# Strassen's scheme for the first dense product of the last two blocks

## Chip, cores and metric

One Trainium2 chip, one core of it. The metric is the device time of one execution in microseconds. A chance or range in the prediction is for the median of such runs.

The engines by the profile's names: PE is the matmul engine (PEld its weight loads), DVE the vector engine, ACT the scalar engine, POOL GpSimd, SP the engine that issues nearly all DMAs. PE writes to PSUM only; the other engines carry results from PSUM to SBUF.

## The reference

Two layers, each an attention of 32 heads (Hedgehog features) followed by a dense block with a squared ReLU, on 2048 rows of 576 columns, all in float32:

```python
def _B_ref(x, w1, b1, w2, b2):             # D = 576, F = 4608
    h = jnp.einsum("bsd,df->bsf", x, w1) + b1
    r = jnp.where(h > zero, h, zero)
    h = r * r
    return jnp.einsum("bsf,fd->bsd", h, w2) + b2

x = A_x
x = x + _A_ref(_layernorm(x), A_wqkv, A_w_phi, A_wo)
x = x + _B_ref(_layernorm(x), B_w1, B_b1, B_w2, B_b2)
x = x + _A_ref(_layernorm(x), A_wqkv, A_w_phi, A_wo)
x = x + _B_ref(_layernorm(x), B_w1, B_b1, B_w2, B_b2)
```

`_A_ref` makes q, k, v, takes per head a small linear map and two softmaxes (of p and of -p) as features, sums features times v over all rows, and gives each row its query's share of these sums, times `wo`.

## The kernel before

**Blocks and order.** The 2048 rows are four blocks of TB = 512 (four tiles t of 128). K's sums need all rows, so a layer has a meeting point (`barrier`); behind it, the blocks are independent. Layer 1 runs them in the order 1, 0, 3, 2. For each block there is a dense block `g_mlp`, and beside it, by `weave`, the attention of the next block (`g_attend`): both are generators, and `weave` traces `rate` steps of the second for each `yield` of the first (36, one for each group f of 128 of the 4608 hidden features). In layer 1 the rate is 1.0, and the last dense block (block 2) has nothing beside it. Tile's planner then orders each engine's instructions: of those that its own estimate holds ready, the one traced first goes first, so the program's order is the priority. The order of an engine is fixed when the kernel is built.

**Precision.** A float32 product is made of three float32r products: each operand is split into a high part (ACT's `Copy` into float32r) and a low part (a subtraction of the high part from the raw value, on DVE or POOL), and hi*hi + hi*lo + lo*hi is summed.

**The dense block, per f** (`g_mlp`, L658 to L763). `first` loads 128 columns of w1 and 128 rows of w2 and splits them (L676, L677 on ACT; L679, L680 on DVE; L681 on POOL), one f ahead. `hidden` (L691) multiplies: D = 576 is four chunks of 128 and a tail of 64, which is stored twice so that one matmul of 128 rows does two of the three products; 5 + 4 + 5 = 14 matmuls with 512 moving columns, into one PSUM bank ("h"). `square` makes ReLU with bias, two squares (L698 to L700, ACT) and the low part (L701, DVE). `second` multiplies the previous f by w2: per tile t three matmuls of 448 columns (L718, `by_rows`), and three of 512 for the last 128 output columns (L709, `features`), into five PSUM banks acc0 to acc4. At the end the accumulators are added to the residual rows from `xm` and written out.

**Attention beside it** (`g_attend`): `g_q` loads the normalized rows back (`unspill`, L350, L351) and multiplies by the folded q weights (L363), 4 steps; `g_soft` (L398 to L407), 4 steps; `g_phi` (L558 to L568), 8 steps; `g_out`, which transposes (L598), multiplies by the sums (L614), then by `wo` (L645), adds the residual (L648) and calls `g_norm` for the dense block's operand. `held` puts the softmax and phi instructions of a step, on DVE, behind the last instruction of the newest `square` (L701). `g_norm` makes mean and variance, scales (L307, L308), transposes each tile on PE (L322, L332) and splits the result into the tiles `xh` and `xl`, which have two buffers.

Tiles in a pool with one tag share its buffers: a new tile of a tag waits until an old one is no longer read. PSUM has eight banks: "h", acc0 to acc4, and two of the tag "w" (`wtile`) for all else in layer 1's blocks.

Of the kernel before, what the change touches and what calls it, by code (L numbers as in the profile page):

```python
# [7 lines left out]
F32 = mybir.dt.float32  # L8
# [13 lines left out]
def layers_kernel(  # L22
# [35 lines left out]
    VW = DH + 1  # L58
    NQ = P // 32
# [13 lines left out]
    wf = dram.tile([D, 2 * D], F32, name="wf")  # L73

# [11 lines left out]
    def drain(gen):  # L86
        for _ in gen:
            pass
# [75 lines left out]
    vslots = [cst.tile([P, H * VW + 32 - VW], F32, name=f"vslot{t}") for t in range(NT)]  # L164
    for vt in vslots:
        nc.gpsimd.memset(vt[:, : H * VW].rearrange("p (h d) -> p h d", d=VW)[:, :, 0:1], 1.0)
        nc.gpsimd.memset(vt[:, H * VW :], 0.0)

# [122 lines left out]

    def g_norm(x_of, dst, name, then=None):

        xd = sb.tile([P, NT, 2, DT], F32, tag="xd", name=f"{name}e", bufs=1)

        def scale(t):
            x = x_of(t)
            stats = sb.tile([P, 2, 6], F32, tag="bns", name=f"{name}s{t}")
            mv = sb.tile([P, 2], F32, tag="bnm", name=f"{name}m{t}")
            rstd = sb.tile([P, 1], F32, tag="rstd", name=f"{name}d{t}")  # L300
            for h in range(2):
                nc.vector.bn_stats(stats[:, h, :], x[:, h * HP : (h + 1) * HP])
            nc.vector.bn_aggr(mv, stats.rearrange("p a b -> p (a b)"))
            nc.gpsimd.tensor_scalar(rstd, mv[:, 1:2], EPS, None, op0=ALU.add)
            nc.gpsimd.tensor_tensor(rstd, rstd, mhalf, op=ALU.pow)
            xn = sb.tile([P, KC * P], F32, tag="xn", name=f"{name}n{t}")
            nc.vector.tensor_scalar(xn, x[:, : KC * P], mv[:, 0:1], rstd, op0=ALU.subtract, op1=ALU.mult)  # L307
            nc.vector.tensor_scalar(xd[:, t], x[:, KC * P :].unsqueeze(1).to_broadcast([P, 2, DT]),  # L308
                                    mv[:, 0:1], rstd, op0=ALU.subtract, op1=ALU.mult)
            if then:  # L310
                then(t, x)
            return xn
# [139 lines left out]
    def sums_operands(layer):  # L452
        kv = sums[layer]["kv"]
        zb = cst.tile([P, 2, D], F32, name=f"zb{layer}", tag="zb")
        kbh = cst.tile([GW, 2, NG, GW], F32R, name=f"kbh{layer}", tag="kbh")
        kbl = cst.tile([GW, 2, NG, GW], F32R, name=f"kbl{layer}", tag="kbl")
# [116 lines left out]
    def g_out(layer, b, ph, dst, name, parts=1, pause=None, behind=None):  # L573
# [81 lines left out]
        yield from g_norm(x_after, dst, f"{name}n", keep)  # L655
# [109 lines left out]

    def load_x(b):
        def get(t):
            x = sb.tile([P, D], F32, tag="x", name=f"x0_{b}_{t}", bufs=5)
            nc.sync.dma_start(x, x_in[b * TB + t * P : b * TB + (t + 1) * P])
            return x  # L770
        return get

    def g_attend(layer, b, x, raws, dst, name, behind=None):
# [9 lines left out]
        yield from g_out(layer, b, ph, dst, name, behind=behind and behind["last"])  # L783
# [63 lines left out]
    for layer in range(2):  # L847
# [4 lines left out]
        for i, b in enumerate(order):  # L852
            n = f"{layer}_{b}"
            nxt = {}
            keep = {}

            def g_back(i=i, prev_rows=prev_rows, keep=keep, nxt=nxt, nxt_raws=nxt_raws):
# [16 lines left out]
                if i + 1 < NB:  # L874
                    yield from g_attend(layer, order[i + 1], None, nxt_raws, nxt, f"a{layer}_{order[i + 1]}",
                                        dense if i == 0 else None)

            rows = []
            weave(g_mlp(layer, b, ready, rows, f"m{n}", None if i else dense["turned"]), g_back(), 1.0 if layer or i == 0 else 1.5)
# [37 lines left out]
```

## Time and profile before

| what | us |
|---|---|
| median of 3 runs (2570.54 to 2573.32) | 2571.38 |
| profiled execution, its own time | 2570.54 |
| its span (first to last instruction) | 2568.5 |
| layer 1, dense block 1 with attention of block 0 | 1510 to 1780 |
| dense block 0 with attention of block 3 | 1780 to 2056 |
| dense block 3 with attention of block 2 | 2056 to 2331 |
| dense block 2 alone | 2331 to 2568 |

A profile shows for each engine when an instruction ran and what it waited for. "Busy" of PE is the time covered by matmuls, whose ends are modelled; the distance from one matmul's start to the next is the better measure of its cost. An idle engine costs nothing unless the end waits for it, so the first question to each view is which engine has no idle time in the stage at hand.

### The profile page before, as it was taken

Reading aid. Unit: us, or ns where it says so; the run is one execution under the profiler, and the core shown is the slowest. Engines: PE = TensorE matmul, PEld = TensorE weight load, DVE = VectorE, ACT = ScalarE, POOL = GpSimd, SP = SyncE. Lnnn points to the kernel's source line nnn. Section 1 sums busy time; section 2 is a strip of 40 time slices with the busy share of each in tenths; the row PEclk is TensorE's granted clock in tenths of the full one; section 3 lists DMA queues with packets and bytes.
Section 4 is the critical chain, followed back from the end, with each engine's and each line's share of the span. In section 5 each row is a group of like instructions: output and inputs, shape, how many; then the busy total and the mean of one; then the engine's idle time right before and its main releaser. Section 6 shows DMA issues by size and latency. Waiting matters only on the chain.

```text
span 2568.5 us, 41275 instructions
## 1 busy us (share of the span) xinstructions
PE 2525.1 (98%) x15456; PEld 2230.4 (87%) x15456; DVE 1456.0 (57%) x2246; ACT 1235.5 (48%) x2061; POOL 634.9 (25%) x645
## 2 busy tenths in 40 slices
PE   8998999999999999999999999999999999999999
PEld 8998888888888888888888988888888888888887
DVE  7778844456665467556434788444663458444333
ACT  4344554445554455545544445535555445534544
POOL 3444311113222133223111433121231213121111
PEclk9999999999999999999999999999999999999999
DMA  8103333354333533343333123334432343234332
GB/s 251 57 23 92 102 111 91 109 185 128 92 93 113 172 126 97 88 133 103 110 101 101 43 90 108 106 103 158 128 103 84 108 160 107 84 101 130 99 101 77
DMA packets 298018, 280.59 MB, mean 109 GB/s; under 512 B 28186, under 2 KB 238362, under 8 KB 295770
## 3 DMA queue, kind: packets, MB, share of 16 engines
q1 hardware_dynamic: 296560, 275.26, 35.3%
q10 hardware_dynamic: 1258, 2.70, 0.3%
q8 instruction: 121, 1.98, 0.3%
q14 instruction: 79, 0.65, 0.1%
HBM read 246.90 MB, written 30.97 MB: 108 GB/s over the span
## 4 chain that ended last, share of the span: by engine, by line
PE 56%; DVE 3%; ACT 1%; issue 0%; DMA 0%; POOL 0%; DVEq 0%; ACTq 0%; SPq 0%; POOLq 0%
PE m_1ph L691 8%; PE m_0ph L691 6%; PE m_1acc L718 6%; PE m_0acc L718 5%; PE m_2ph L691 5%; PE m_3ph L691 4%; PE m_3acc L718 3%; PE m_2acc L718 3%; PE m_1acc L709 2%; PE m_0acc L709 1%; PE m_2acc L709 1%; PE m_3acc L709 1%; PE a_2po L645 1%; PE t1opo L645 1%; PE k_0kp L363 1%; PE t1pv L363 1%
## 5 line engine op out<-in xcount | busy, mean ns | idle before, releaser
L718 PE MATMUL m_1acc<-m_1s,m_1hb 128*128 128x448 f32 x864 | 199.3, 366 | 1.5 <-DVE m_1hb L701 1.5
L718 PE MATMUL m_0acc<-m_0s,m_0hb 128*128 128x448 f32 x864 | 199.4, 366 | 1.3 <-DVE m_0hb L701 1.3
L718 PE MATMUL m_3acc<-m_3s,m_3hb 128*128 128x448 f32 x864 | 199.7, 366 | 1.0 <-DVE m_3hb L701 1.0
L718 PE MATMUL m_2acc<-m_2s,m_2hb 128*128 128x448 f32 x864 | 199.4, 366 | 1.3 <-DVE m_2hb L701 1.3
L691 PE MATMUL m_0ph<-a_0nh,m_0h 128*128 128x512 f32 (+1 forms) x760 | 192.8, 383 | 0.2 <-DVE m_0h L679 0.2
L691 PE MATMUL m_2ph<-a_2nh,m_2h 128*128 128x512 f32 (+1 forms) x760 | 192.0, 382 | 0.2 <-DVE m_2h L679 0.2
L718 PEld LDWEIGHTS m_0acc<-m_0s,m_0hb 128*128 128x128 f32 x864 | 161.9, 188 | 23.2 <-DVE m_0hb L701 2.2
L718 PEld LDWEIGHTS m_1acc<-m_1s,m_1hb 128*128 128x128 f32 x864 | 162.0, 188 | 22.9 <-DVE m_1hb L701 2.3
L718 PEld LDWEIGHTS m_2acc<-m_2s,m_2hb 128*128 128x128 f32 x864 | 161.9, 188 | 22.8 <-DVE m_2hb L701 2.2
L718 PEld LDWEIGHTS m_3acc<-m_3s,m_3hb 128*128 128x128 f32 x864 | 161.8, 188 | 22.6 <-DVE m_3hb L701 1.4
L679 DVE TENSOR_TENSOR m_2h<-m_2r,m_2h 128x640 fp32r<-128x640 f32 x72 | 61.8, 858 | 181.6 <-ACT m_2h L676 179.5
L691 PEld LDWEIGHTS m_2ph<-a_2nh,m_2h 128*128 128x128 f32 x760 | 136.9, 188 | 26.7 <-DVE m_2h L679 0.7
L691 PEld LDWEIGHTS m_0ph<-a_0nh,m_0h 128*128 128x128 f32 x760 | 136.6, 188 | 26.8 <-DVE m_0h L679 0.7
L679 DVE TENSOR_TENSOR m_3h<-m_3r,m_3h 128x640 fp32r<-128x640 f32 x72 | 65.6, 912 | 157.1 <-ACT m_3h L676 147.9
L679 DVE TENSOR_TENSOR m_1h<-m_1r,m_1h 128x640 fp32r<-128x640 f32 x72 | 64.9, 903 | 155.4 <-ACT m_1h L676 149.3
L679 DVE TENSOR_TENSOR m_0h<-m_0r,m_0h 128x640 fp32r<-128x640 f32 x72 | 64.7, 899 | 153.9 <-ACT m_0h L676 148.5
L681 POOL TENSOR_TENSOR m_2s<-m_2r,m_2s 128x128 fp32r<-128x128 f32 x72 | 60.7, 844 | 361.7 <-ACT m_2s L677 343.2
L681 POOL TENSOR_TENSOR m_0s<-m_0r,m_0s 128x128 fp32r<-128x128 f32 x72 | 59.5, 826 | 351.7 <-ACT m_0s L677 318.5
L681 POOL TENSOR_TENSOR m_3s<-m_3r,m_3s 128x128 fp32r<-128x128 f32 x72 | 58.5, 813 | 341.8 <-ACT m_3s L677 321.8
L681 POOL TENSOR_TENSOR m_1s<-m_1r,m_1s 128x128 fp32r<-128x128 f32 x72 | 59.7, 829 | 322.4 <-ACT m_1s L677 312.8
L698 ACT ACTIVATE m_3hr<-m_3ph,b1t 128x512 f32<-128x512 f32 x72 | 49.4, 687 | 186.6 <-PE m_3ph L691 181.7
L698 ACT ACTIVATE m_0hr<-m_0ph,b1t 128x512 f32<-128x512 f32 x72 | 49.4, 686 | 176.2 <-PE m_0ph L691 173.6
(1507 smaller groups left out, 6381.0 us busy)
## 6 DMA issues: line engine op xcount, KB each, us to landing
m_3r<-in_B_w SPq DMA_DIRECT2D x72, 288.0 KB
m_2r<-in_B_w SPq DMA_DIRECT2D x72, 288.0 KB
m_0r<-in_B_w SPq DMA_DIRECT2D x72, 288.0 KB
m_1r<-in_B_w SPq DMA_DIRECT2D x72, 288.0 KB
m_3r<-in_B_w SPq DMA_DIRECT2D x72, 256.0 KB
m_2r<-in_B_w SPq DMA_DIRECT2D x72, 256.0 KB
m_0r<-in_B_w SPq DMA_DIRECT2D x72, 256.0 KB
m_1r<-in_B_w SPq DMA_DIRECT2D x72, 256.0 KB
```

Source lines behind the costliest of these rows:

```text
L363: nc.tensor.matmul(pt[:, :HP], a, m, start=(k == 0), stop=(k == len(ops) - 1))
L645: nc.tensor.matmul(pt[:, :HP], a, m[:w, g], start=(g == 0 and k == 0), stop=(g == NG - 1 and k == 2))
L679: nc.vector.tensor_sub(l1, r1, h1.bitcast(F32))
L681: nc.gpsimd.tensor_sub(s2[:, D + R : 2 * D], r2[:, R:], s2[:, R:D].bitcast(F32))
L691: nc.tensor.matmul(ph[:, cols], a, m, start=(k == 0), stop=(k == len(ops) - 1))
L698: nc.scalar.activation(hr, ph, AF.Relu, bias=b1t[:, f : f + 1])
L709: nc.tensor.matmul(acc[KC], a, m, start=(f == 0 and k == 0), stop=(f == NF - 1 and k == 2))
L718: nc.tensor.matmul(acc[t][:, :R], a[:, rows], m, start=(f == 0 and k == 0), stop=(f == NF - 1 and k == 2))
```

## The change

The dense blocks of blocks 3 and 2 are no longer two runs of `g_mlp` but one generator, `g_pair`. For two groups f0, f1 (a pass k, 18 of them) and both blocks, the first product is a 2x2 by 2x2 product of blocks: the weights w1 cut in K into halves of 288 (HP) and in features into f0, f1 (a11, a12 for f0; a21, a22 for f1); the normalized rows cut in K and into block 3 (b11, b21) and block 2 (b12, b22). The scheme (Winograd's form of Strassen's) makes seven products:

- of weights: a11, a12, s1 = a21+a22, s2 = s1-a11, s4 = a12-s2, s3 = a11-a21, a22
- of rows: b11, b21, t1 = b12-b11, t2 = b22-t1, b22, t3 = b22-b12, t4 = b21-t2

and sums them in three PSUM banks: bx = a11*b11, then + s2*t2, + s3*t3, + a22*t4; by = a12*b21, then s4*b22; bz = s1*t1. Each product has 7 matmuls of 512 columns: K of 288 is two chunks of 128 and 32 rows, which stand three times in one operand of 96 rows (TP) so that one matmul does all three partial products.

Second products: block 3's follows in the passes as before (`second`); block 2's squared hidden values are written to DRAM (`hd`, 36 tiles of 256 KB), and when block 3 is done, its 36 second products follow alone with w2 loaded once more.

The rows' sums t1 to t4 are made where the rows are normalized: `g_norm_first` (block 3) writes its operand to DRAM (`pth`, `ptl`, `ptt`); `g_norm_second` (block 2) loads it and makes the sums (`combine`: DVE and POOL) and their splits. For that, both attentions must be done before `g_pair`: they now both run beside block 0's `g_mlp`, at 2.2 steps an f in place of 1.0. The weights' sums and splits are made by `split_pair` one pass ahead. Many operands live in buffers of other tags (`zb`, `xd`, `kbh`, `kbl`, the v slots, `E`, `ft`, `whi`, `wraw`, `x`, `qk`).

The core of the diff:

```diff
+    def new_slot(t, name, dtype=F32):
+        return cst.tile([P, NC * P], dtype, name=name, tag=f"vslot{t}")
...
+    def g_norm_halves(x_of, name, then, main, tail):
+        xd = sb.tile([P, NT, 2 * TP], F32, tag="xd", name=f"{name}e", bufs=1)
+        xns = []
+        for t in range(NT):
+            x = x_of(t)
+            mv, rstd = moments(x, t, name)
...
+            yield
+        for t in range(NT):
+            pt = wtile(f"{name}p{t}")
...
+            main(t, p4)
+            yield
+            if t % 2:
+                pt = wtile(f"{name}p{NT}{t}")
+                p3 = pt[:TP].rearrange("p (a n) -> p a n", a=2)
+                for a in range(2):
+                    for i in range(2):
+                        nc.tensor.transpose(p3[:, a, i * P : (i + 1) * P],
+                                            xd[:, t - 1 + i, a * TP : (a + 1) * TP], ident)
+                tail(t // 2, p3)
+                yield
...
+        def combine(new, c11, c21):
+            b12, b22 = new
+            temps = [sb.tile([P, D], F32, tag="x", name=f"{name}u{i}", bufs=5) for i in range(2)]
...
+            nc.vector.tensor_sub(t1, b12, c11[0])
+            if len(c11) > 1:
+                nc.vector.tensor_sub(t1, t1, c11[1])
+            nc.vector.tensor_sub(t2, b22, t1)
+            nc.vector.tensor_copy(t3, b12)
+            nc.vector.tensor_sub(t3, b22, t3)
+            nc.gpsimd.tensor_sub(t4, c21[0], t2)
+            if len(c21) > 1:
+                nc.gpsimd.tensor_add(t4, t4, c21[1])
+            return (("b22", b22), ("t1", t1), ("t2", t2), ("t3", t3), ("t4", t4))
+        def main(t, p4):
...
+            for k, src in combine((p4[:, 0], p4[:, 1]), *old):
+                hi, lo = (p[:, :, rows] for p in ops[k][:2])
+                nc.scalar.activation(hi, src, AF.Copy)
+                (nc.vector if k == "b22" else nc.gpsimd).tensor_sub(lo, src, hi.bitcast(F32))
...
+    def g_pair(layer, blocks, x, after, name):
...
+            def split(key, src):
+                op = homes[key].rearrange("p (c n) -> p c n", c=NC)
+                hi, lo = op[:, : HK + 1], op[:, HK + 1 :]
+                nc.scalar.activation(hi, src, AF.Copy)
+                nc.vector.tensor_sub(lo, src[:, :HK], hi[:, :HK].bitcast(F32))
+                band = slice(2 * TW, 3 * TW)
+                nc.gpsimd.tensor_sub(hi[band, HK], src[band, HK], hi[band, HK].bitcast(F32))
+                wops[k, key] = (hi, lo)
+
+            split("a11", a11)
+            split("a12", a12)
+            nc.gpsimd.tensor_add(ss[0], a21, a22)
+            split("s1", ss[0])
+            nc.gpsimd.tensor_sub(ss[1], ss[0], a11)
+            split("s2", ss[1])
+            yield
+            nc.gpsimd.tensor_sub(ss[3], a12, ss[1])
+            split("s4", ss[3])
+            nc.gpsimd.tensor_sub(ss[2], a11, a21)
+            split("s3", ss[2])
+            split("a22", a22)
...
+        def product(k, ps, key, op, start):
+            hi, lo = wops.pop((k, key))
+            xh, xl, xtail = x[op]
+            ms = [(hi[:, c], xh[:, c]) for c in range(HK)] + [(hi[:TP, HK], xtail)]
+            ms += [(hi[:, c], xl[:, c]) for c in range(HK)]
+            ms += [(lo[:, c], xh[:, c]) for c in range(HK)]
+            for i, (a, m) in enumerate(ms):
+                nc.tensor.matmul(ps, a, m, start=start and i == 0, stop=i == len(ms) - 1, skip_group_check=True)
...
+        drain(split_pair(0, load_pair(0)))
+        raw = load_pair(1)
+        for k in range(NP):
+            f0, f1 = 2 * k, 2 * k + 1
+            prep = split_pair(k + 1, raw) if k + 1 < NP else iter(())
...
+            load_wide(f0)
+            product(k, bx, "a11", "b11", True)
+            product(k, by, "a12", "b21", True)
+            z = sb.tile([P, TB], F32, tag="hr", name=f"{name}z{f0}", bufs=2)
+            nc.scalar.activation(z, by, AF.Copy)
+            nc.vector.scalar_tensor_tensor(z, bx, bias(f0), z, op0=ALU.add, op1=ALU.add)
+            nc.scalar.activation(z, z, AF.Relu)
+            square(f0, z)
+            product(k, bz, "s1", "t1", True)
+            next(prep, None)
+            product(k, bx, "s2", "t2", False)
...
+            nc.scalar.activation(v, bz, AF.Copy)
+            nc.vector.tensor_add(u, bx, v)
+            product(k, by, "s4", "b22", True)
+            product(k, bx, "s3", "t3", False)
+            nc.vector.scalar_tensor_tensor(u, by, bias(f0), u, op0=ALU.add, op1=ALU.add)
+            nc.vector.scalar_tensor_tensor(v, bx, bias(f1), v, op0=ALU.add, op1=ALU.add)
+            nc.scalar.activation(u, u, AF.Relu)
+            nc.scalar.activation(u, u, AF.Square)
+            nc.sync.dma_start(hd[f0], u)
+            keep_high(f1, v)
+            if k:
+                second(f0 - 1)
+            load_wide(f1)
+            product(k, bx, "a22", "t4", False)
+            drain(prep)
+            z = sb.tile([P, TB], F32, tag="hr", name=f"{name}z{f1}", bufs=2)
+            nc.scalar.activation(z, bx, AF.Relu, bias=bias(f1))
+            square(f1, z)
+            if k + 2 < NP:
+                raw = load_pair(k + 2)
+            second(f0)
+            yield
+        last_rows(0)
...
+        for f in range(NF, 2 * NF - 1):
+            second(f)
+            if f + 2 < 2 * NF:
+                load_wide(f + 2)
+                load_high(f + 2)
+            yield
+        last_rows(1)
...
         for i, b in enumerate(order):
...
+            if layer and i == 2:
+                drain(g_pair(layer, order[2:], operands, rows, f"m{n}"))
+                break
...
+                if layer and i == 1:
+                    for j, norm in ((2, g_norm_first), (3, g_norm_second)):
+                        yield from g_attend(layer, order[j], None, None, operands, f"a{layer}_{order[j]}", None, norm)
...
-            weave(g_mlp(layer, b, ready, rows, f"m{n}", None if i else dense["turned"]), g_back(), 1.0 if layer or i == 0 else 1.5)
+            weave(g_mlp(layer, b, ready, rows, f"m{n}", None if i else dense["turned"]), g_back(), 1.0 if i == 0 else 2.2 if layer else 1.5)
```

The functions used there and not shown: `load_pair` loads 256 columns of w1 in two halves of K (the 32 tail rows four times, side by side in 128 partitions); `load_wide` loads and splits 128 rows of w2, as `first` did; `square`, `features`, `by_rows`, `second` and `last_rows` are those of `g_mlp` with an index for the block; `load_high` loads a tile of `hd` and splits it.

246 lines of the change are left out of this document (226 added, 20 removed).

## The prediction

> **What bounds the kernel now.** I read the page first: busy shares, then the chain of waits.
>
> ```profile
> span 2568.5 us, 41275 instructions
> PE 2525.1 (98%) x15456; PEld 2230.4 (87%) x15456; DVE 1456.0 (57%) x2246; ACT 1235.5 (48%) x2061; POOL 634.9 (25%) x645
> ```
>
> PE is busy for 98% of the span. Then the stages that change, by windows: layer 1's second, third and fourth blocks (columns: us, then PE, PEld, DVE, ACT, POOL busy, clock, DMA share, GB/s).
>
> ```profile
> 1780.00:2056.00 276.00, 275.63 (x1404) 240.62 (x1403) 149.50 (x226) 136.39 (x221) 59.27 (x61) 1.00 0.39 119
> 2056.00:2331.00 275.00, 273.89 (x1395) 238.69 (x1394) 147.46 (x226) 133.61 (x218) 58.33 (x62) 1.00 0.36 109
> 2331.00:2568.00 237.00, 232.41 (x1097) 200.56 (x1095) 82.45 (x124) 112.97 (x180) 32.83 (x36) 1.00 0.35 104
> ```
>
> The first two hold a dense block and the next block's attention, the last a dense block alone. And all that PE waited for after 1510 us, by the view of waits (total, times, longest):
>
> ```profile
> PE m_1acc L718 <- DVE m_1hb L701: 1.0, 1, 1.0
> PE t1onp L322 <- DVE t1onn L307: 0.9, 1, 0.9
> PE a_2np L322 <- DVE a_2nn L307: 0.7, 1, 0.7
> PE a_3np L322 <- DVE a_3nn L307: 0.4, 1, 0.4
> PE a_0np L322 <- DVE a_0nn L307: 0.4, 1, 0.4
> ```
>
> 3.4 us in 1058: these stages are bound by PE's own work. So matmuls taken out come off the end one for one, as long as the other engines still stay hidden. Every new stall comes on top.
>
> **Step 1, the first product: -28.9 us.** For two groups f of 128 hidden features and two blocks, `hidden` issues 2x2x14 = 56 matmuls; seven `product` calls issue 7x7 = 49, of the same 128x512 form (K is 256 + 96 stacked rows instead of 512 + 64 doubled). The chain shows one `hidden` of 14, in two alternating lengths:
>
> ```profile
> 2401.28 3.26 PE m_2ph L691 x14
> 2407.66 3.17 PE m_2ph L691 x14
> ```
>
> Mean 3.215 us, 0.2296 each. 18 passes x 7 = 126 fewer: 28.9 us. The second products stay: 72 x 15 matmuls.
>
> **Step 2, transposes: +1 us.** The tail of K is now transposed by halves: 8 transposes a block for 4, so 8 more for two blocks.
>
> ```profile
> 1783.10 0.66 PE a_0np L322 x4
> ```
>
> 0.165 each, 1.3 us by this row and less within a run of them: I take 1.
>
> **Step 3, two attentions within one dense block: +18 us.** Both attentions now run beside block 0's `g_mlp` at 2.2 steps an f. One attention has 39 steps (4 q, 4 softmax, 8 phi, 13 in `g_out`, 10 in the norm), two 78, and 36 x 2.2 = 79. PE's work only moves. DVE's is the question; four windows of one answer:
>
> ```profile
> 2360.00:2550.00 190.00, 190.00 (x871) 163.27 (x870) 64.32 (x90) 94.63 (x150) 27.02 (x30) 1.00 0.33 95
> 1827.00:1905.00 78.00, 78.00 (x357) 66.66 (x356) 65.03 (x90) 42.28 (x66) 28.47 (x25) 1.00 0.35 103
> 663.00:725.00 62.00, 60.92 (x289) 52.21 (x288) 58.52 (x83) 35.96 (x55) 24.97 (x21) 1.00 0.38 110
> 1470.00:1480.00 10.00, 6.39 (x33) 6.16 (x32) 10.00 (x17) 1.30 (x4) 5.00 (x4) 0.66 0.32 90
> ```
>
> Row one is the dense block alone: 30 f's, so 6.33 us of PE and 64.32/30 = 2.14 us of DVE each. Row two is softmax and phi of one attention at 1.0 step an f: 65.03 - 78/6.33 x 2.14 = 38.7 us of DVE for the attention. Softmax, phi and the empty step behind are 13 steps: at 2.2 they span 5.9 f's, 37.4 us of PE, while DVE needs 38.7 + 5.9 x 2.14 = 51.3. It is short by 13.9 us. `held` puts each step's DVE work behind the last square of its f, and the following f's weight and square subtractions queue behind it; those are late next, and PE waits for them as it did at L701. PE can run ahead by about one `hidden` (3.2 us) to one f (6.3), and instructions of coming f's slip into gaps of the chain. I take 9 a time, 18 for two. Lower bound, row three: at 1.5 steps an f, DVE busy 58.52 of 62, PE lost 62 - 60.92 = 1.1: 2 us for two. Upper: all of it, 28. The attention's ACT work there is 42.28 - 12.3 x 94.63/30 = 3.5 us and its POOL work 28.47 - 12.3 x 27.02/30 = 17.4, both far under 37.4. In `g_out` DVE has room and the order recovers, but a PE idle time is not won back.
>
> **Step 4, between the two attentions: 0 us.** Normalized block 3 goes out by three transfers (2.4 MB), and only then does block 2's come in (2.3 MB), since xh and xl have two buffers and block 0 holds one. What one load takes, from its issue on SP to the first q product:
>
> ```profile
> 1777.35 0.38 SPq L350 DMA_DIRECT2D a_3uh<-xth  x1
> 1790.25 0.42 PE L363 MATMUL a_3qp<-a_3q0h,a_3uh 128*128 128x288 f32 x2
> ```
>
> 13 us at most, perhaps 20 with the store: three f's of `g_mlp`, whose matmuls can fill it; the four q steps (14 us of PE) then come without f's between. Without that cover it costs 13. On SP the loads of coming f's (issued one f ahead) must get past these waits.
>
> **Step 5, the hand-over to `g_pair`: +7 us.** The old hand-overs cost PE 0.4 and 0.7 (L322 above). Now, behind the last step, `xd` must be free before half of the first weights loads, `full` (in vslot0 and 1, the homes of a11 and a12) must be read, and POOL has a queue: a `main` gives it six 128x256 operations, four mains and two tails 26, then split_pair(0) four sums and seven bands. POOL's prices (lines; mean ns behind the busy time):
>
> ```profile
> L652 POOL TENSOR_TENSOR a_3x<-a_3x,b2t 128x576 f32<-128x576 f32 x4 | 5.7, 1432 | 2.9 <-DVE a_3ne L308 2.9
> L249 POOL TENSOR_TENSOR w0v0l<-fv,w0v0h 128x288 fp32r<-128x288 f32 x5 | 4.0, 796 | 6.9 <-ACT w0v0h L248 6.9
> L681 POOL TENSOR_TENSOR m_2s<-m_2r,m_2s 128x128 fp32r<-128x128 f32 x72 | 60.7, 844 | 361.7 <-ACT m_2s L677 343.2 <-issue 18.4
> L304 POOL TENSOR_SCALAR n_0d<-n_0m 128x1 f32<-128x1 f32 x4 | 0.9, 221 | 6.8 <-DVE n_0m L303 6.8
> ```
>
> At 0.8 the 26 take 21 us in a stretch that PE crosses in 6/2.2 f's, 17 us, and a few transposes: 2 to 4 late. Then s1 needs two bands, a sum, ACT's copy and its band, about 3.5 us; each further sum with copy and band about 2 against the 1.6 of a product. a11 and a12 (3.2 us) cover part. I take 8, less one old hand-over: 7; from 1 (all ready in time) to 13 (26 x 0.8 - 17, 3.5 and 7 x 0.844, uncovered).
>
> By the clock: row four above is a stretch with one PE wait of 3.6 us (L500, the longest of all); the granted clock there is 0.66, 3.4 us lost in 10. The Trainium skill (TensorE: Matmul & The Clock Gate, What's actually happening) says that a window of about 3.4 us without work halves the clock; the trace agrees, and by that rule one unbroken wait of 7 us would make the sum 3 higher.
>
> **Step 6, the pair loop: +5 us.** A pass has 49 + 30 matmuls: 49 x 0.2296 + 2 x (6.33 - 3.215) = 17.5 us. Against it (rows of the dense block alone, of the fold, and of a block's end):
>
> ```profile
> L701 DVE TENSOR_TENSOR m_2hb<-m_2hr,m_2hb 128x512 fp32r<-128x512 f32 x30 | 20.8, 693 | 10.8 <-ACT m_2hr L700 10.8
> L680 DVE TENSOR_TENSOR m_2s<-m_2r,m_2s 128x448 fp32r<-128x448 f32 x30 | 18.8, 626 | 20.3 <-ACT m_2s L677 20.3
> L241 DVE TENSOR_TENSOR w0k0l<-fo,w0k0h 128x288 fp32r<-128x288 f32 x5 | 2.2, 445 | 0.0
> L676 ACT ACTIVATE m_2h<-m_2r 128x640 fp32r<-128x640 f32 x30 | 21.9, 729 | 0.0
> L677 ACT ACTIVATE m_2s<-m_2r 128x576 fp32r<-128x576 f32 x30 | 20.6, 686 | 20.5 <-PE m_2acc L709 19.5 <-DVE m_2hb L701 1.0
> L699 ACT ACTIVATE m_2hb<-m_2hr 128x512 fp32r<-128x512 f32 x30 | 18.6, 621 | 0.0
> ```
>
> DVE: 7 x 0.42 (128x256, just under L241) + 2 x 0.63 + 6 x 0.69 = 8.3 us. ACT: 7 x 0.53 (128x384, down the slope from L676 to L699) + 2 x 0.69 + 12 x 0.63 = 12.7. POOL: 4 x 1.0 (128x384, between L249 and L652) + 2 x 0.84 + 7 bands of 32x128, from 0.22 (L304) to 0.84: 7.2 to 11.6. Nobody exceeds PE. s2 must wait until DVE has read bx: copy 0.62 + 0.69 and handovers against s1's 1.6 us, so it has no slack; I take 0.3 a pass, 5 us, from 0 to 18 x 0.69 = 12. Queued behind that DVE read are u, v and coming weights, a pass ahead. SP: 1.9 MB a pass, 106 GB/s, against 279 shown below; a store of `hd` waits for ACT with coming loads behind it, also a pass early.
>
> POOL and DVE get in each other's way; from the timeline:
>
> ```profile
> 689.02 1.44 POOL L558 TENSOR_TENSOR a_0m<-a_0Q0e,zb 128x576 f32<-128x576 f32 x1
> 689.20 1.74 DVE L680 TENSOR_TENSOR m_2s<-m_2r,m_2s 128x448 fp32r<-128x448 f32 x1
> ```
>
> The subtraction that takes 0.63 took 1.74: POOL began 0.18 us before, and it ended 0.48 after POOL. The Trainium skill (SBUF — State Buffer, Who interferes with whom) has the rule: a DVE instruction with two inputs in SBUF and a GpSimd instruction that reads SBUF exclude each other. The trace agrees; this is rival B's mechanism.
>
> **Step 7, block 2's second product alone: +2 us.** An f now has 3.1 us of PE against ACT 0.69 + 0.62, DVE 0.63 + 0.69 in turn behind it, 2.6 in all: it fits by half a microsecond, with 544 KB per 3.1 us, 179 GB/s, below what this row shows:
>
> ```profile
> 1780.00:1800.00 20.00, 19.63 (x139) 18.59 (x138) 11.09 (x23) 8.35 (x16) 4.46 (x6) 1.00 0.82 279
> ```
>
> From 0 to 36 x 0.3 = 10. **Sum:** -28.9 + 1 + 18 + 0 + 7 + 5 + 2 = +4. The profiled execution took 2570.54 us, 2 more than its span, and lies 0.8 below the median: 2574.5, as a median 2575.4.
>
> **Rivals.** A, the order absorbs DVE's shortage as at 1.5 steps an f (1.1 each): step 3 costs 2, the sum is -12, 2559. For it speaks row three, where DVE had nothing to spare and PE lost almost nothing; against it, that there DVE's need (38.7 + 9.8 f's x 2.14 = 59.7) still fitted into 62. B, the shared access binds the pair loop: DVE's two-input work (7 x 0.42 + 2 x 0.63 + 2 x 0.69 = 5.6 us) excludes POOL's. With bands at 0.84 and sums at 1.43 POOL has 13.3; 18.9 against 17.5 is 1.4 a pass, 25 for 18 in place of 5: 2595. It decides once POOL is above 11.9. C, the transfers between the attentions aren't covered, since SP stands in wait while block 0's weights queue behind: +13, 2588.
>
> **The numbers.** Forecast 0.45 (2575, its own range 2564 to 2588), A 0.33, B 0.14, C 0.08. About 0.2%, 5 us, can be told from no change. Faster by more: A nearly whole and a bit of the forecast, 0.34; within: 0.20; slower: 0.46. The range takes A with less in steps 5 and 6 (2549) and most of B: 2549 to 2600.
>
> **What would show it.** Step 1: 882 first-product matmuls at 0.23 for 1008. Step 3: PE waits for DVE L701's and L679's likes, twice, about 9 us each, in block 0's softmax and phi; none, and A is right. Step 4: idle before the second q products. Step 5: one PE stall of 5 to 10 us before s1, ended by POOL or ACT. Step 6: passes of 17.5 to 18 us; 19 with POOL over 70% busy is B. Step 7: 3.1 us an f. The prediction is wrong if step 3 or 5 costs nothing, or if a wait not listed costs over 10 us.

## The result and the profile after

| | us |
|---|---|
| before, median of 4 runs (2570.54 to 2573.32) | 2571.79 |
| after, median of 4 runs (2591.81 to 2594.93) | 2593.59 |
| ratio, with its 95% interval | 1.0084 (1.0067 to 1.0102) |
| span of the profiled execution, before and after | 2568.5 and 2590.1 |

The change makes the kernel 22 us slower, 0.8%, and clear of the runs' spread. In the experiments below, one execution of t4_dve took 4970 us where its other four took 2581 to 2584; it is left out of that kernel's ratio, and its cause is open. The first page of the profile after, span and busy times:

```profile
span 2590.1 us, 41423 instructions
PE 2519.7 (97%) x15282; PEld 2211.0 (85%) x15282; DVE 1533.6 (59%) x2408; ACT 1266.7 (49%) x2177; POOL 797.6 (31%) x869
```

PE has 174 instructions fewer than before. That is the 126 of step 1, plus 56 since block 3's and block 2's first two f's had been multiplied in halves (2 x 2 x 14 more matmuls) and the pair has none of these, less the 8 transposes of step 2. The work has gone as forecast; the span has grown in spite of it. All that PE waited for over 1 us after 1510 us, from the view of waits (total, times, longest):

```profile
PE m_0ph L708 <- DVE m_0h L696: 7.4, 4, 2.7
PE a_2pt L615 <- DVE a_2Q3e L585: 5.0, 1, 5.0
PE a_2np L805 <- DVE a_2nl L904: 3.3, 1, 3.3
PE m_0py L771 <- DVE a_2nl L904: 2.7, 1, 2.7
PE m_3px L988 <- DVE m_3wv L954: 2.5, 1, 2.5
PE m_3py L988 <- ACT m_3wv L953: 1.9, 1, 1.9
PE m_3px L988 <- DVE m_3u L1089: 1.5, 1, 1.5
PE a_2np L805 <- DVE a_2nh L877: 1.3, 1, 1.3
PE m_3py L988 <- POOL m_3wv L956: 1.1, 1, 1.1
```

The first two rows belong to softmax and phi of the two attentions, the others to the norm that feeds the pair and to the pair's first pass. The windows put them in their places (us, then PE, PEld, DVE, ACT, POOL busy, clock, DMA share, GB/s):

```profile
1820.00:1840.00 20.00, 17.28 (x74) 14.40 (x73) 19.06 (x24) 12.81 (x19) 8.71 (x7) 0.91 0.17 47
1840.00:1860.00 20.00, 16.10 (x63) 12.28 (x62) 19.45 (x34) 6.77 (x11) 10.06 (x8) 0.91 0.21 63
2000.00:2020.00 20.00, 18.68 (x85) 15.62 (x84) 19.88 (x33) 10.15 (x17) 9.50 (x8) 1.00 0.28 79
2020.00:2040.00 20.00, 14.98 (x62) 11.93 (x61) 13.29 (x20) 6.05 (x11) 5.67 (x5) 0.83 0.35 98
2120.00:2140.00 20.00, 13.25 (x58) 9.35 (x56) 16.60 (x40) 11.77 (x30) 14.31 (x21) 0.94 0.31 91
2140.00:2160.00 20.00, 13.66 (x42) 9.14 (x42) 13.11 (x23) 8.07 (x16) 14.67 (x19) 0.72 0.46 148
2400.00:2420.00 20.00, 20.00 (x90) 16.45 (x89) 9.13 (x14) 10.52 (x19) 8.22 (x10) 1.00 0.35 105
2480.00:2500.00 20.00, 20.00 (x97) 17.92 (x96) 9.63 (x13) 7.25 (x12) 5.53 (x7) 1.00 0.68 213
```

Rows one to four are softmax and phi of the first and the second attention: DVE is full where PE has gaps (in row four until 2026, where PE's wait of 5.0 us for it ends). Rows five and six are the hand-over, where no engine is full and PE, at 0.72 of its clock in the second, does 42 matmuls in 20 us; row seven, a stretch of the pair loop, has 90. The last two rows, the pair loop and block 2's second product alone, have no gap at all.

Busy times hide the slow matmuls, so the account below goes by starts: the distance from each matmul's start to the next, less the median distance of the same form in the same trace, summed over a stretch. It holds idle time and lowered clock together. In the other stretches behind 1510 us, before and after differ by less than 1.5 us each.

| lost by PE, us | before | after | of after's, idle |
|---|---|---|---|
| softmax and phi, first attention, 1825 to 1860 | 0.3 | 11.1 | 6.6 |
| between, 1860 to 2000 | 0.2 | 1.3 | 0.0 |
| softmax and phi, second attention, 2000 to 2040 | 0.2 | 9.8 | 6.4 |
| hand-over, 2080 to 2200 | 0.4 | 26.1 | 18.4 |

### The profile page after: what moved, and what is told of

The parts are those of the page before. It is cut to its first block, busy times and chain, and to the rows that moved or that the text cites. A ratio compares the mean times of both kernels' runs of the same rounds, so it can differ in the third digit from the quotient of the medians.

```text
span 2590.1 us, 41423 instructions
## 1 busy us (share of the span) xinstructions
PE 2519.7 (97%) x15282; PEld 2211.0 (85%) x15282; DVE 1533.6 (59%) x2408; ACT 1266.7 (49%) x2177; POOL 797.6 (31%) x869
## 4 chain that ended last, share of the span: by engine, by line
PE 50%; DVE 7%; POOL 2%; issue 1%; ACT 1%; DMA 0%; DVEq 0%; POOLq 0%; SPq 0%; ACTq 0%
PE m_1ph L708 8%; PE m_1acc L735 6%; PE m_0ph L708 5%; PE m_3px L988 4%; PE m_0acc L735 4%; PE m_3acc L1017 3%; PE m_3acacc L1017 2%; PE m_3py L988 2%; PE m_1acc L726 2%; PE m_0acc L726 1%; PE m_3acacc L1007 1%; PE m_3pz L988 1%; PE m_3acc L1007 1%; PE m_3ach L1017 1%; PE t1opo L662 1%
## 5 line engine op out<-in xcount | busy, mean ns | idle before, releaser
L708 PE MATMUL m_0ph<-a_0nh,m_0h 128*128 128x512 f32 (+1 forms) x760 | 199.7, 389 | 8.0 <-DVE m_0h L696 7.9
L696 DVE TENSOR_TENSOR m_1h<-m_1r,m_1h 128x640 fp32r<-128x640 f32 x72 | 64.9, 902 | 155.4 <-ACT m_1h L693 155.4
L696 DVE TENSOR_TENSOR m_0h<-m_0r,m_0h 128x640 fp32r<-128x640 f32 x72 | 66.6, 926 | 122.0 <-ACT m_0h L693 119.4
L715 ACT ACTIVATE m_1hr<-m_1ph,b1t 128x512 f32<-128x512 f32 x72 | 49.5, 687 | 171.5 <-PE m_1ph L708 171.5
L977 DVE TENSOR_TENSOR m_3s<-m_3r,m_3s 128x448 fp32r<-128x448 f32 x72 | 49.5, 688 | 95.3 <-ACT m_3s L976 93.5
L735 PE MATMUL m_2acc<-m_2s,m_2hb 128*128 128x448 f32 x432 | 99.7, 366 | 1.3 <-DVE m_2hb L718 1.3
L735 PE MATMUL m_3acc<-m_3s,m_3hb 128*128 128x448 f32 x432 | 99.6, 366 | 0.9 <-DVE m_3hb L718 0.9
L978 POOL TENSOR_TENSOR m_3s<-m_3r,m_3s 128x128 fp32r<-128x128 f32 x72 | 58.0, 805 | 134.5 <-ACT m_3s L976 127.9
L708 PE MATMUL m_2ph<-a_2nh,m_2h 128*128 128x512 f32 (+1 forms) x380 | 97.3, 384 | 0.3 <-DVE m_2h L696 0.3
L708 PE MATMUL m_3ph<-t0onh,m_3h 128*128 128x512 f32 (+1 forms) x380 | 95.7, 382 | 0.1
L708 PE MATMUL m_1ph<-t1onh,m_1h 128*128 128x512 f32 (+1 forms) x380 | 95.7, 382 | 0.0
L708 PE MATMUL m_1ph<-a_1nh,m_1h 128*128 128x512 f32 (+1 forms) x380 | 95.3, 381 | 0.0
L1017 PE MATMUL m_3acc<-m_3s,m_3hb 128*128 128x448 f32 x432 | 94.4, 366 | 0.1
L735 PEld LDWEIGHTS m_2acc<-m_2s,m_2hb 128*128 128x128 f32 x432 | 80.8, 188 | 12.3 <-DVE m_2hb L718 2.2
```

Of the source, the lines that this page charges most:

```text
L696: nc.vector.tensor_sub(l1, r1, h1.bitcast(F32))
L708: nc.tensor.matmul(ph[:, cols], a, m, start=(k == 0), stop=(k == len(ops) - 1))
L715: nc.scalar.activation(hr, ph, AF.Relu, bias=b1t[:, f : f + 1])
L735: nc.tensor.matmul(acc[t][:, :R], a[:, rows], m, start=(f == 0 and k == 0), stop=(f == NF - 1 and k == 2))
L977: nc.vector.tensor_sub(s2[:, D : D + R], r2[:, :R], s2[:, :R].bitcast(F32))
L978: nc.gpsimd.tensor_sub(s2[:, D + R : 2 * D], r2[:, R:], s2[:, R:D].bitcast(F32))
```

## The experiments

Three questions: is the seventh's saving earned (step 1); do the 20.9 us of softmax and phi come from their density (step 3); and what makes the hand-over cost 26 us (step 5). Lost times in this part are from the same account; medians are compared with the changed kernel's 2593.6 unless another is named. The kernels ran in several sessions on several chips; the kernel before, which ran in each, had medians of 2571.3 to 2572.7 there, so a difference of medians below some 1.5 us tells nothing. And Tile's planner orders every kernel anew, so that an edit can also move instructions that it doesn't name.

### Eight products in place of seven

```diff
-            hi, lo = wops.pop((k, key))
+            hi, lo = wops[k, key]
...
-            product(k, bz, "s1", "t1", True)
+            for _ in range(2):
+                product(k, bz, "s1", "t1", True)
```

> The changed kernel with the product s1 x t1 of every pass made twice, the second over the first: eight block products in place of seven, with all of the rest of the change. Theory (step 1: the pair loop is bound by PE, and the seventh's saving of 126 matmuls of 0.23 us is earned in full): 28.9 us more, 2620 to 2624 us, passes of 19.3 us. Rival (a pass is held by POOL, ACT, or the exchange of PSUM banks, and a product less is worth only part): under 20 us more, below 2614 us.

Measured: 2621.5 us (2619.2 to 2622.4), 27.9 more. From the fourth on a pass takes 19.20 to 19.25 us, against 17.71 to 17.78. The 1.48 us that a pass grows are 0.13 short of the 1.61 that seven matmuls take there. The timeline of the pass at 2290 shows why, first in the changed kernel (start, us, engine, line; x2 is two matmuls): the last two of s1, then those of s2.

```profile
2290.82 0.62 PE L988 MATMUL m_3px<-a_2nb11h,m_3wv 128*128 128x512 f32 x2
...
2295.20 0.62 PE L988 MATMUL m_3pz<-a_2nt1h,m_3wv 128*128 128x512 f32 x2
2295.68 0.73 PE L988 MATMUL m_3px<-a_2nh,m_3wv 128*128 128x512 f32 x2
2296.26 0.39 PE L988 MATMUL m_3px<-a_2nt2t,m_3wv 96*128 96x512 f32 x1
...
2308.53 0.62 PE L988 MATMUL m_3px<-a_2nb11h,m_3wc_9h 128*128 128x512 f32 x2
```

s2's first two begin 0.48 after s1's last two and take 0.58 until the next, where others take 0.45 to 0.46: some 0.14 us of waiting, since DVE must have read bx. With s1 made twice it is gone:

```profile
2273.24 0.62 PE L988 MATMUL m_3px<-a_2nh,m_3wv 128*128 128x512 f32 x2
2273.69 0.40 PE L988 MATMUL m_3px<-a_2nt2t,m_3wv 96*128 96x512 f32 x1
```

So the pair loop is bound by PE, a product is worth its matmuls, and step 1's saving was earned in full. What the change adds besides is some 50 us.

### Softmax and phi less dense

```diff
-        yield from held(g_soft(raws, er, name))
-        yield from held(g_phi(layer, er, ph, name, True))
+        for g in (g_soft(raws, er, name), g_phi(layer, er, ph, name, True)):
+            for _ in held(g):
+                for _ in range(slots):
+                    yield
...
-            weave(g_mlp(...), g_back(), 1.0 if i == 0 else 2.2 if layer else 1.5)
+            weave(g_mlp(...), g_back(), 1.0 if i == 0 else 2.87 if layer else 1.5)
```

`slots` is 2 for the two attentions beside block 0 and 1 elsewhere.

> The changed kernel, with an empty step behind each of the 24 softmax and phi steps of the two attentions and 2.87 steps an f in place of 2.2: the softmax and phi steps then come at 1.43 an f, all others at 2.87. Theory (step 3: DVE falls short where these steps come at 2.2 an f, 11 us in the first attention and 9.5 in the second): 15 to 18 of the 20.6 us come back, 2575 to 2579 us, and the stretches of softmax and phi show PE busy over 18.5 of 20 us at a clock above 0.95. Rival (the loss belongs to having two attentions in one dense block, at whatever density): 2590 to 2595, the idle time only moves to other steps.

Measured: 2575.0 us (2573.0 to 2577.9), 18.6 less. The windows of this kernel, same columns:

```profile
1820.00:1840.00 20.00, 19.15 (x88) 16.13 (x87) 18.35 (x24) 12.42 (x18) 7.54 (x8) 1.00 0.24 66
1840.00:1860.00 20.00, 19.79 (x90) 16.63 (x89) 18.80 (x31) 9.48 (x15) 8.77 (x9) 1.00 0.38 113
2000.00:2020.00 20.00, 20.00 (x94) 17.25 (x93) 19.59 (x29) 10.01 (x16) 10.01 (x8) 1.00 0.37 103
```

DVE is nearly as full, but PE has work and its clock. The two stretches lose 1.5 and 0.2 us, in place of 11.1 and 9.8; between them 3.1 in place of 1.3; the hand-over 25.7, as before. The rival, that the idle time would only move, falls.

### The hand-over: four single causes

In the changed kernel PE begins the pair's first product at 2136.84, and then stands, or runs at the low clock, until 2152; the timeline of PE, with idle time and releaser in brackets:

```profile
2118.53 0.63 PE L805 MATMUL a_2np<-ident,a_2nn 128*128 128x128 f32 x4 [3.27 <-DVE a_2nl L904]
2135.41 0.66 PE L771 MATMUL m_0py<-ident,m_0yt 128*128 128x128 f32 x4 [2.71 <-DVE a_2nl L904]
2136.84 0.73 PE L988 MATMUL m_3px<-a_2nb11h,m_3wv 128*128 128x512 f32 x2 [0.77 <-ACT m_3wv L953]
2141.76 1.22 PE L988 MATMUL m_3px<-a_2nb11h,m_3wv 128*128 128x512 f32 x2 [2.52 <-DVE m_3wv L954]
2144.83 1.22 PE L988 MATMUL m_3py<-a_2nb21h,m_3wv 128*128 128x512 f32 x2 [1.85 <-ACT m_3wv L953]
2147.77 1.05 PE L988 MATMUL m_3py<-a_2nb21l,m_3wv 128*128 128x512 f32 x2
```

Behind it stand four queues. POOL's and ACT's, at the norm's last tiles and at the first sum of pair 0:

```profile
2133.15 0.72 POOL L893 TENSOR_TENSOR a_2nu<-a_2nu,a_2nb21l 128x256 f32<-128x256 f32 x1
2135.88 0.72 POOL L904 TENSOR_TENSOR a_2nt3l<-a_2nu,a_2nt3h 128x256 fp32r<-128x256 f32 x1
2144.39 1.00 POOL L961 TENSOR_TENSOR m_3s<-m_3r,m_3r 128x384 f32<-128x384 f32 x1 [5.74 <-DMA m_3r<-in_B_w]
```

```profile
2133.90 0.42 ACT L903 ACTIVATE a_2nt4h<-a_2nu 128x256 fp32r<-128x256 f32 x1 [2.45 <-POOL a_2nu L893]
2134.53 0.36 ACT L903 ACTIVATE a_2nh<-a_2np 128x256 fp32r<-128x256 f32 x1
```

ACT stands 2.45 us until POOL has made t4; behind that copy comes b22's (`a_2nh<-a_2np`), which PE's next transposes need, as b22 lies in a PSUM bank (which, in this kernel, only ACT and DVE read). POOL itself works without a pause from 2126.5 to 2136.6, does two operations more, and then stands 5.74 us for the raw weights. Those are SP's:

```profile
2131.30 0.38 SPq L928 DMA_DIRECT2D m_3r<-in_B_w  x1
2131.74 0.45 SPq L930 DMA_DIRECT2D m_3r<-in_B_w  x1
2132.29 5.28 SPq L774 DMA_DIRECT2D m_0x<-xm  x4
2137.62 0.42 SPq L930 DMA_DIRECT2D m_3r<-in_B_w  x1
2139.21 2.52 SPq L780 DMA_DIRECT2D out<-m_0x  x4
2141.78 0.92 SPq L930 DMA_DIRECT2D m_3r<-in_B_w  x2
```

The first row is the half of pair 0's raw weights that goes to `xd`, issued when the last transposes have read it (2130.66 in the timeline of PE). Of its four loads of 32 rows the first goes at once, the others behind block 0's loads and stores (the stores wait for DVE's additions); the last two at 2141.78. The fourth queue is DVE's, here from the chain that ended last:

```profile
2140.76 0.61 DVE m_0x L779
2141.37 0.34 DVE m_3wv L954
```

The second row is the low part of a11, for which PE waits the 2.52 us. ACT's copy of a11 is there at 2136.8, but DVE works through the norm's tails and block 0's last eight additions, from 2134.93 on without a pause, before it comes to it. No kernel here moves this by itself, nor the access that DVE and POOL share: at 2135.71 a tail's subtraction (L877) took 1.17 us beside POOL's work, and the next one 0.41.

So there are four suspects that an edit can reach: t4 on POOL; ACT's order; the raw half in `xd`; POOL's sums. One kernel for each:

```diff
# t4_dve: t4 on DVE
-            nc.gpsimd.tensor_sub(t4, c21[0], t2)
+            nc.vector.tensor_sub(t4, c21[0], t2)
...
-                nc.gpsimd.tensor_add(t4, t4, c21[1])
+                nc.vector.tensor_add(t4, t4, c21[1])
# raw0_kb: other homes of the raw weights
-            tags = ((cst, "zb"), (sb, "xd")) if k % 2 == 0 else ((cst, "kbh"), (cst, "kbl"))
+            tags = ((cst, "zb"), (sb, "xd")) if k % 2 else ((cst, "kbh"), (cst, "kbl"))
# t4_late: ACT's copy of t4 behind the next main's copies
+            for k, src in new[:4]:
+                last = put(rows, k, src)
+            late.append((rows, *new[4]))
+            with tc.issue_after(last.ins):
+                while len(late) > (t < NT - 1):
+                    put(*late.pop(0))
# sums_dve: pair 0's and 1's sums on DVE
+            adder = nc.vector if k < 2 else nc.gpsimd
-            nc.gpsimd.tensor_add(ss[0], a21, a22)
+            adder.tensor_add(ss[0], a21, a22)
```

> The changed kernel with the two operations that make t4 on DVE in place of POOL, in the four mains and two tails of the norm that feeds the pair. Theory a (the hand-over's 26 us start with POOL's chain, which ACT's copy of t4 and all behind it wait for): 4 to 8 us come back, 2585 to 2589 us, and the waits of the transposes L805 (3.5 us) and L771 (2.7 us) on DVE's low part of b22 go. Theory b (what ends the hand-over is the raw weights' second half, which stands behind block 0's last loads and stores on SP's queue): the time stays within 2 us of 2593, as a12 is as late as before.

> The changed kernel with the raw weights of even and odd pairs exchanged: pair 0's go to kbh and kbl, which are free before the norm, and pair 1's to zb and xd. Theory b (a12 waits for the half in xd, 6.3 us of PE idle at 2138 to 2144): 4 to 7 us come back, 2586 to 2589 us, and the first matmul of a12 starts before 2140. Theory c (POOL's sums and bands of pair 0 come one after the other and are late by themselves): a12 is early, but s1 waits the longer; under 2 us come back, 2591 to 2594.

> Both together: t4 on DVE and pair 0's raw weights in kbh and kbl. If the two waits lie one behind the other, what each brings adds up: 8 to 14 us, 2579 to 2585 us. If one hides the other, the pair brings more than the sum of the two alone, or no more than the better of the two: then the difference from that sum says which.

> The changed kernel with ACT's copy of each main's t4 queued behind the four copies of the next main (the last one's behind its own); t4 and its low part stay on POOL, with as many operations as before. Theory a1 (what costs is that ACT, which takes its instructions in turn, stands at t4's copy until POOL is there, and b22's copy, which frees the PSUM bank, and block 0's squares stand behind it): 5 to 9 us come back, 2584 to 2589 us, most of what t4 on DVE brought. Theory a2 (POOL has more to do than the stretch is long, and pair 0's sums start late for that): under 2.5 us come back, 2591 to 2594, as POOL ends no earlier.

> The changed kernel with the four sums of block weights of pairs 0 and 1 (eight operations of 128x384, 1.0 to 1.3 us each) on DVE in place of POOL; t4 stays on POOL. Theory a2 (all that POOL has to do between the first main and the end of pass 0, 43 us of 56, sets the hand-over, and t4 is only the part that was tried): 9 us taken off POOL bring what t4's 10 operations brought or somewhat less, 5 to 10 us, 2584 to 2589 us. Rival f (t4's place in the norm mattered, ahead of block 0's last f's; in pass 0 it is the raw weights' transfer and ACT's order that set the time): under 3 us come back, 2591 to 2594, with DVE's waits in place of POOL's.

| kernel | median, us | ratio to before, interval | lost in the hand-over |
|---|---|---|---|
| changed | 2593.6 | 1.0067 to 1.0102 | 26.1 |
| t4_dve | 2582.9 | 1.0025 to 1.0054 | 17.7 |
| raw0_kb | 2590.3 | 1.0053 to 1.0086 | 23.6 |
| raw0_t4 | 2583.0 | 1.0027 to 1.0057 | 17.3 |
| t4_late | 2592.9 | 1.0062 to 1.0092 | 25.6 |
| sums_dve | 2590.2 | 1.0049 to 1.0082 | 25.1 |

Only the kernels with t4 on DVE stand clear of the changed one: 10.7 us less, more than I expected. The other three single edits bring 0.7 to 3.4 us by the medians, with intervals that overlap the changed kernel's; no execution of raw0_kb or sums_dve was as slow as the fastest of the changed kernel (2590.7 at most, against 2591.8), so that some 3 us are likely there. What the traces say of each:

In t4_dve the first product starts at 2130.65, 6.2 us earlier, and the raw half is no longer late: `xd` comes free 5 us earlier, so that SP issues its loads at 2126.25, all four of 32 rows together, ahead of block 0's loads. That the raw half adds nothing on top (raw0_t4) follows from it. So one mechanism made several of the waits: POOL is late in the norm, and the norm's end, `xd`, SP's order and the raw weights are late behind it.

In t4_late the waits that were to go are gone: the first product starts at 2131.75, and s1 at 2143.21, 6.3 us before the changed kernel (2149.48). Two later waits take that back:

```profile
2135.59 0.80 PE L999 MATMUL m_3px<-a_2nb11t,m_3wv 96*128 96x512 f32 x1 [3.11 <-POOL m_3wv L967]
...
2152.00 0.79 PE L999 MATMUL m_3py<-a_2nh,m_3wa 128*128 128x512 f32 x1 [6.09 <-ACT m_3z L1090]
```

In the second, PE waits for ACT's copy that frees the bank `by`. In the changed kernel that copy comes at 2149.88, ahead of pair 1's; here the planner has put three copies of pair 1 ahead of it, at which ACT stands 0.43, 1.34 and 1.34 us for POOL's sums. The last of them and the copy:

```profile
2150.94 0.52 ACT L964 ACTIVATE m_3wc_1l<-m_3s 128x384 fp32r<-128x384 f32 x1 [1.34 <-POOL m_3s L977]
2151.37 0.58 ACT L1090 ACTIVATE m_3z<-m_3py 128x512 f32<-128x512 f32 x1
```

The time, 0.7 us less, is theory a2's, but not its reason, that POOL ends no earlier: POOL begins pair 1's sums at 2146.20, 4.3 us before the changed kernel (2150.51). Nor does it refute theory a1 (the copy of t4 in ACT's order): what was won up to s1 was lost again to another order on ACT. The two stay undecided. In sums_dve a2's number is missed (3.4 us for 5 to 10; rival f had under 3): POOL is relieved of 9 us, but only behind the raw weights, which come as late as before:

```profile
2144.54 0.66 POOL L957 TENSOR_TENSOR m_3wv<-m_3r,m_3wv 32x128 fp32r<-32x128 f32 x1 [6.31 <-ACT m_3wv L954]
```

By t4_dve and sums_dve it isn't the sum of POOL's work from first main to last pass that counts, but its work ahead of the norm's end; behind that the raw weights are the later ones, and POOL stands idle. In raw0_kb it is the other way round: a12 starts at 2139.71, before 2140 as theory b has it, but 3.3 us come back for 4 to 7, and s4 waits 2.7 us for ACT. (The 6.3 us that its expectation gives to PE were ACT's wait for the raw half; PE's own idle time there is 2.52 and 1.85.) The sums and the raw half relieved together, without t4, weren't tried.

### Earlier in block 0, with and without t4

`early` is the spread kernel at 3.2 steps an f, `early_t4` adds t4 on DVE, `early_sums` the eight sums as well; `mid_t4` is early_t4 at 3.0.

> The spread kernel (2575 us) at 3.2 steps an f in place of 2.87: the last mains and tails of the norm come three to four f's before block 0's end, with POOL still making t4. Theory d (the hand-over costs 25 us because 26 operations of POOL and their copies come in the last two or three f's, with nothing of PE left to lie under them): with 20 us more of PE work behind them most of it goes, and pair 0's sums move forward too; 10 to 18 us less, 2557 to 2565 us. Rival e (POOL's chain in each main holds ACT, the PSUM bank and block 0's squares wherever it comes): the waits only move forward, 2571 to 2577 us. Softmax and phi come at 1.6 an f, at most 3 us worse than at 1.43.

> The early kernel with t4 on DVE as well. Theory d: little is left for it, at most 3 us below the early kernel, 2555 to 2562 us. Rival e: the full 8 us that t4 on DVE brought in the hand-over come here too, 8 to 10 us below the early kernel.

> The early_t4 kernel (2564 us) at 3.0 steps an f in place of 3.2. Softmax and phi come at 1.5 an f, the projections at 3.0; the last mains come two f's before block 0's end. If the 5 us of PE idle that early_t4 has in 1860 to 1990 come from the density of 3.2, about 3 of them come back and the hand-over, with fewer f's behind it, costs up to 3 more: 2561 to 2566 us. If two f's of cover are too few for the norm, the hand-over costs 5 or more again: 2567 to 2570 us.

> The early_t4 kernel (2564 us) with the same eight sums on DVE. Theory a2: POOL, busy 18.7 and 17.9 of 20 us at 2120 to 2160, is still what the first passes wait for, and 2 to 5 us come back, 2559 to 2562 us. Rival: DVE, which has the exchange of the PSUM banks to do in time, holds these up instead; no gain, or up to 4 us lost, 2563 to 2568 us.

| kernel | median, us | ratio to before, interval | lost in the hand-over |
|---|---|---|---|
| spread | 2575.0 | 1.0001 to 1.0020 | 25.7 |
| early | 2572.7 | 0.9995 to 1.0014 | 20.2 |
| early_t4 | 2564.0 | 0.9959 to 0.9982 | 9.7 |
| mid_t4 | 2568.4 | 0.9973 to 0.9992 | 17.0 |
| early_sums | 2562.6 | 0.9945 to 0.9975 | 6.7 |

Theory d, more matmuls behind the norm to cover POOL, falls: the early kernel gains 2.3 us. Two parts hide in that. The hand-over loses 5.5 us less than in the spread kernel, far from most of its 25; and the attentions, now at 1.6 softmax and phi steps an f, lose 5.9 more (10.7 for 4.8, from 1825 to 2040), where 3 at most were expected. The norm's first transposes come at 2078.03, 15 us earlier, and the waits go with them: 5.5 us before the norm's transposes (L805, L813), and 3.4 us for one of block 0's squares. That is the longest of this row, whose other four waits lie in the attentions:

```profile
PE m_0acc L735 <- DVE m_0hb L718: 7.9, 5, 3.4
```

Before it the timeline of ACT and DVE has POOL's t4 again; the square's low part (L718) stands on DVE behind t4's tail, and that behind ACT's copy of it:

```profile
2106.99 0.42 ACT L876 ACTIVATE a_2nt4t<-a_2nu 96x256 fp32r<-96x256 f32 x1 [1.52 <-POOL a_2nu L891]
```

```profile
2107.43 0.41 DVE L877 TENSOR_TENSOR a_2nt4t<-a_2nu,a_2nt4t 32x256 fp32r<-32x256 f32 x1 [1.06 <-ACT a_2nt4t L876]
2107.86 0.69 DVE L718 TENSOR_TENSOR m_0hb<-m_0hr,m_0hb 128x512 fp32r<-128x512 f32 x1
```

With t4 on DVE as well 8.7 us come back, as rival e has it. In mid_t4 the hand-over costs 7.3 more than at 3.2, and 3.1 us are won in the attentions (10.5 to 7.4); the time is that of the expectation's second half. Its reason, that the norm has too little cover, the trace doesn't show: the norm's transposes wait 1.1 us in all, and PE waits in the pair's first passes (3.1 and 1.8 us for DVE, L1080 and L1093). The sums on DVE bring 1.4 us here by the medians and 2.8 by the ratios to the kernel before, within the intervals: neither a2 nor its rival is settled. early_t4 and early_sums are faster than both kernels: 0.3 and 0.4% below before, 30 and 31 us below the changed kernel.

### The lowered clock

A third of what is lost in the three stretches is slow matmuls, not idle time (26.1 - 18.4 = 7.7 us in the hand-over). Are they a cost of their own?

```diff
+        if layer and name == f"m1_{order[1]}":
+            fill = ps_a.tile([P, TB], F32, tag="h", name=f"{name}fill")
+            b11 = operands["b11"][0]
+            for i in range(24):
+                nc.tensor.matmul(fill, b11[:, 0, :P], b11[:, 1], start=True, stop=True)
         pt = wtile(f"{name}py")
...
         prepare()
+        dst.update(ops)
```

> The spread kernel (2575 us) with 24 matmuls of 128x512 more, whose output nothing reads, at the end of block 0, most of them just ahead of the transposes L771 that wait 5.6 us there. Theory (the clock falls because PE stands idle, and 8 us of the hand-over's 25 are matmuls at the lower clock): the 5.5 us of added matmuls lie in the wait, the clock stays above 0.9 from 2120 to 2140 (0.59 in the spread kernel), and 3 to 6 us come back, 2569 to 2572 us. Rival (the clock falls for another reason, or the wait is not there to be filled): the clock is as low as before and the time is the same or up to 6 us longer, 2575 to 2581 us.

Measured: 2574.3 us (2573.6 to 2575.2) against the spread kernel's 2575.0. One window, in the spread kernel and then with the added matmuls:

```profile
2120.00:2140.00 20.00, 14.27 (x38) 9.65 (x39) 14.07 (x28) 8.91 (x21) 15.21 (x20) 0.59 0.51 160
```

```profile
2120.00:2140.00 20.00, 14.47 (x52) 9.96 (x51) 15.48 (x30) 10.79 (x24) 16.03 (x20) 0.89 0.53 173
```

The wait was there to be filled: 5.5 us of matmuls cost nothing, and the clock follows (0.59 to 0.89). But the time doesn't, 0.7 us within the intervals. PE's slow matmuls there cost 6.6 us in place of 10.1, but its idle time and the filling together are 17.6 in place of 15.6: it meets the later waits sooner, and POOL still waits 2.37 us for the raw weights. So neither expectation holds whole: the clock rose as the theory has it, and the time stayed as the rival has it. At this place the low clock is a result of the waiting, and mostly no cost beside it; the other places weren't filled.

## Why the prediction was right, and where it was off

The direction and the range were right. The size was not: +4 us by the sum, +22 measured. The range was 51 us wide, and slower had a chance of only 0.46. The 2593.6 lie outside the forecast's own 2564 to 2588 and beside rival B's 2595, but B's mechanism is not what happened: that nearness is chance. By the steps:

- **Step 1 (-28.9):** right. 126 matmuls fewer, and the eighth product put back costs 27.9.
- **Step 2 (+1):** 8 transposes more are in the count of instructions; their cost wasn't measured by itself.
- **Step 3 (+18):** right in place, cause and size. 11.1 and 9.8 us, with DVE full, and 18.6 us of the total come back once the density is lowered. The named waits are there too: the subtraction on the weights (L679 before, L696 now) four times, 7.4 us. One wait as long as 5.0 us was not named: the attention's own transposes (L615), for phi's last product on DVE (L585).
- **Step 4 (0):** right, 1.3 us, none of it idle.
- **Step 5 (+7, at most 13):** the mis-sized term; 26.1 less the 1.1 of the two old hand-overs, 25. That POOL is late by a few us was right (t4 off it brings the most that any single edit did), and its price was not too low: the 26 operations took 0.73 us each in the median, for 0.8. Missing was what is late next: the norm's end releases `xd`, the raw weights' second half is then late behind block 0's transfers on SP's queue (a12 begins 8.0 us behind a11, where a product takes 1.6), and only then do pair 0's sums begin, on the same POOL; DVE comes late to a11's low part besides. The prediction named `xd` as a suspect and gave it no price, so the bound of 13 had none of it either. The step's sign didn't come either: there is no one stall of 5 to 10 us that POOL or ACT ends, but many, the three longest (3.3, 2.7 and 2.5) ended by DVE, two of them behind ACT and POOL. Its 3 us for one unbroken wait of 7 stood outside the sum. (The wait at L500 that it read the clock from is not the longest of all: L462 has one of 3.8 us.)
- **Step 6 (+5):** the sum is right, its parts differ. A pass takes 17.73 where 17.48 was the matmuls' part of the forecast, 0.25 x 15 = 3.8 us from the fourth pass on. s2's lack of slack costs 0.14 a pass and not 0.3; the rest is the matmuls' own pace: a product 1.61 us for 1.607, and a second product of 15 matmuls 3.14 (block 2's f's alone follow each other at that distance) for 3.115.
- **Step 7 (+2):** 0.9 us, 35 x (3.14 - 3.115); no wait.

With what the kernel before lost in the same stretches taken off (0.5 and 0.2), the sum is -28.9 + 1 + 20.4 + 1.1 + 25 + 3.8 + 0.9 = 23.3; the span grew by 21.6. The 1.7 left over are not accounted for.

**Rivals.** A fell: at 2.2 the order absorbed part of DVE's shortage (20.9 us lost, 13.0 of them idle, of the 28 of step 3), not nearly all (2). At 1.43 the same sum leaves DVE short by 4 us a time at most, so that the spread kernel doesn't test how much an order can absorb. B fell: passes of 17.73 us, not 18.9, and POOL busy 8.2 to 13.5 of 20 us, 10.9 in the mean, in the eleven windows from 2200 to 2420, where 14 were asked for. C fell with step 4.

## What to carry to other kernels

When work is moved beside a stage with one bounding engine, price the other engines over the few us in which the moved steps come, not over the stage: at 2.2 steps an f DVE's shortage cost PE 10 us a time, at 1.43 under 2. At a hand-over, follow each late result through what it releases (a buffer, a transfer on an in-order queue, the next engine's first operation) and add the links up, since one engine late at the head made several kinds of waits here. Relieving a later link alone brought little here (0.7 to 3.4 us): look in the trace for the first engine of the chain that works without a pause. And read the order of the engines again after a single edit, since the next wait may come from an instruction that the edit never named.

## What was not expected of the hardware

- How long PE stands at a time doesn't decide the granted clock alone. In the changed kernel a wait of 2.72 us, which ends at 1834.29, took the clock to 0.91 over 1820 to 1840 (3.4 us at 0.50), with no other wait of PE in these 20 us; one of 3.27 us, which ends at 2118.53, left it at 1.00 from 2115 to 2137. In the hand-over it was 0.72 over 2140 to 2160, behind waits of 2.71, 0.77, 2.52, 1.85 and 1.12 us in a row: two matmuls at 2147.77 start 0.86 before the next two, where the pair loop has 0.46, and the full pace was back at 2151.4, 4 us after the last of these waits. The Trainium skill (TensorE: Matmul & The Clock Gate, What's actually happening) names an idle window of about 3.4 us. By this trace a single shorter wait can be enough; what else decides, the runs don't show.
- A band of 32x128 cost POOL 0.45 us at best, a subtraction of 128x128 (L978) 0.46: a quarter of the partitions saved nothing.
